# A planner's cost table replaced by durations read from a trace, in a one-core attention and feed-forward kernel

## The chip, the cores and the metric

The kernel runs on one core of a Trainium2 chip. The metric is the device time of one execution in microseconds (us). Three runs of the kernel before gave 1211.63, 1219.78 and 1224.26 us; their median, 1219.78 us, is the time before.

## What is computed

Four batches of 448 tokens, 12 heads of 64, in float32: an attention with a sigmoid in place of the softmax, and behind it two feed-forward parts on all 1792 tokens.

```python
# attention, for each batch and head
scores = q @ k.T / sqrt(64) - log(448)
x = sigmoid(scores) @ v                         # heads side by side: [1792, 768]
# first part
xn = x / sqrt(mean(x * x) + 1e-6) * rms_g
g, val = xn @ w_gate, xn @ w_val                # [768, 1536] each
x = (g * sigmoid(g) * val) @ w_out              # [1536, 768]
# second part
h = x @ w_in                                    # [768, 2048]
out = (h - tanh(h)) @ w_out2                    # [2048, 768]
```

All weights arrive as float64 words and are turned into float32 on the chip.

## The kernel before

**Products.** Tokens stand on the free axis: a matrix product takes a 128x128 block of weights and the 448 tokens of one batch. An operand is held as two float32r parts, a high one and a low one (the rest), and a product is three matmuls: high with high, high with low, low with high (L706 to L711). Nearly all matmuls of the kernel, 4896 of about 5600, stand on line L708.

**Jobs.** The feed-forward work is a list of 142 jobs, each with a piece of six weight blocks. A job of two batches is 36 matmuls. The phases are Ag and Av (gate and value), B (`w_out`), C (`w_in`) and D (`w_out2`); first the jobs of batches 0 and 1, then those of batches 2 and 3. B and D work on groups of four hidden chunks, so that four blocks make one run into a PSUM bank; a run of Ag, Av and C has six blocks.

**Conversion of a piece** (`conv`, L339 to L403): a DMA brings 768 KB (tile `raw`, two buffers); ACT makes the lowest mantissa bits (L374); DVE makes the sign (L377); DVE or ACT drops the sign (L381 or L380); DVE rebiases the exponent (L383); DVE joins the words (L387, tile `cv`, two buffers); DVE or ACT casts to the high part (L283, tile `whl`, four buffers); DVE or GpSimd (POOL) subtracts for the low part (L400).

**Epilogues** (L649 to L678): when a run of blocks is done, ACT takes a sigmoid (L654) or a tanh (L662) of the PSUM bank, DVE multiplies, subtracts or adds (L655, L658, L663, L672), and `parts` splits the result for the next phase: a cast on ACT or DVE (L283, `unit<-unit`), a subtraction on POOL or DVE (L645).

**Attention.** Batches 0 and 1 come first, two heads at a time (scores L468 and L469, values L500 and L508). The heads of batches 2 and 3 are spread over the jobs of batches 0 and 1: scores, sigmoid in place (L475), cast (L283), low part (L540), values (L552 to L555), then the squares and their sum (L576, L583). When a batch's heads are done, `norm` (L589) forms 1/rms: PE sums (L598), DVE (L612), POOL's power (L614), DVE (L603), PE (L608), ACT (L618). `x_chunk` (L627) then scales the rows (L630 on POOL or DVE, L633 on ACT, L634 on DVE).

**What sets the order.** Nothing above is issued at once. Each piece of work is given to a `Plan` (L62) with its engines and, for each, a duration in ns and whether it holds the port that DVE and POOL share. `Plan.issue` walks the work with a clock for each engine: of the pieces whose start lies within `SOON` (300 ns) of the soonest, it takes the one named first, on the engine that can start it first (L174 to L178), and advances that engine's clock by the duration. The pieces are then issued in the order of their planned starts (L204). So the durations decide two things: on which engine a piece runs where there is a choice, and where it stands in each engine's queue. On the chip each engine runs its queue in that fixed order and waits where a result isn't there yet; the plan's times themselves are not used.

The durations come from three functions and from numbers written at the call: `act(n)` (L273), `dve(n)` (L276) and `pool(n)` (L279) for n elements per partition, and `MM` (L39) for a matmul of 448 columns.

## Time and profile before

| | |
|---|---|
| median of three runs | 1219.78 us |
| lowest and highest run | 1211.63 and 1224.26 us |
| span of the profiled execution, first to last instruction | 1208.7 us |
| matmuls (PE) busy | 1177.1 us |
| DVE busy | 1049.3 us, 1444 instructions |
| ACT busy | 567.9 us, 852 instructions |
| GpSimd (POOL) busy | 253.1 us, 162 instructions |
| granted TensorE clock, mean | 0.992 of full speed (2.4 GHz) |

The whole time of the profiled execution isn't listed, only its span; the lowest run lies 2.9 us above that span, the median 11.1 us. PE is the engine of the matmuls, and their ends are modelled, so that its busy share alone doesn't tell how well it runs: how many matmuls start in a stretch tells that. A row of the timeline says when an instruction, or a merged group of them, started and how long it took; in square brackets stands for how long the engine was idle before it and who ended that.

### The profile page before, as it was taken

The numbers are of one execution on the slowest core, as the hardware profiler recorded it, in microseconds if no ns is written. First come the engines' busy times: TensorE is split into PE (matmuls) and PEld (weight loads), VectorE is DVE, ScalarE is ACT, GpSimd is POOL, SyncE is SP. The second block draws the span as 40 slices with busy tenths as digits, with TensorE's granted clock in tenths as the row PEclk, the third lists the DMA queues.
The fourth block names the chain that finished last, engine by engine and source line by source line (L and its number), as shares of the span: only waits on it lengthen the run. The fifth ranks groups of instructions, "written<-read, shape, count | busy, mean of one in ns | idle before, by whom it ended". The sixth has DMA issues, their size and how long they took to land.

```text
span 1208.7 us, 15035 instructions
## 1 busy us (share of the span) xinstructions
PE 1177.1 (97%) x5694; PEld 1042.7 (86%) x5694; DVE 1049.3 (87%) x1444; ACT 567.9 (47%) x852; POOL 253.1 (21%) x162
## 2 busy tenths in 40 slices
PE   8999999999997999999999899999999999999998
PEld 4566799989896998898899899999999999999997
DVE  4898899899999898999997999888878899888872
ACT  6876535554642566556554433243343344433330
POOL 0102312023223231222122402202212111111120
PEclk9999999999998999999999999999999999999999
DMA  7655233433333233433354243333333234332312
GB/s 253 221 190 173 69 125 137 140 115 115 126 133 111 69 111 116 137 118 106 105 171 145 84 165 105 131 106 130 105 107 107 74 105 135 127 105 105 109 49 91
DMA packets 39223, 148.86 MB, mean 123 GB/s; under 512 B 4592, under 2 KB 14064, under 8 KB 39152
## 3 DMA queue, kind: packets, MB, share of 16 engines
q1 hardware_dynamic: 39152, 147.92, 35.6%
q8 instruction: 44, 0.72, 0.2%
q14 instruction: 27, 0.22, 0.1%
HBM read 139.64 MB, written 8.26 MB: 122 GB/s over the span
## 4 chain that ended last, share of the span: by engine, by line
PE 59%; DVE 27%; ACT 6%; issue 5%; DMA 2%; POOL 1%; SPq 0%; DVEq 0%; POOLq 0%; ACTq 0%
PE ps L708 53%; DVE raw L383 4%; DVE raw L381 3%; DVE cv L387 3%; DVE unit L540 3%; DVE cv L377 2%; ACT raw L380 2%; DVE unit L645 2%; DVE unit L283 2%; PE ps L500 2%; PE ps L468 1%; PE ps L469 1%; DMA qkr<-in_qkt 1%; ACT cv L374 1%; ACT unit L283 1%
## 5 line engine op out<-in xcount | busy, mean ns | idle before, releaser
L708 PE MATMUL ps<-unit,whl 128*128 128x448 f32 x4680 | 971.7, 366 | 8.9 <-ACT unit L283 3.0
L708 PEld LDWEIGHTS ps<-unit,whl 128*128 128x128 f32 x4680 | 880.3, 188 | 83.2 <-DVE unit L540 5.0
L400 POOL TENSOR_TENSOR whl<-cv,whl 128x768 fp32r<-128x768 f32 x79 | 152.5, 1930 | 643.6 <-DVE whl L283 338.8
L374 ACT ACTIVATE cv<-raw 128x768 uint16<-128x768 uint16 x136 | 148.8, 1096 | 209.0 <-DVE whl L400 81.0
L383 DVE TENSOR_SCALAR raw<-raw 128x768 uint16<-128x768 uint16 x136 | 149.2, 1097 | 31.4 <-ACT raw L380 28.2
L387 DVE SCALAR_TENSOR_TENSOR cv<-raw,cv 128x768 uint32<-128x768 uint32 x136 | 143.4, 1054 | 7.9
L283 ACT CAST unit<-unit 128x448 fp32r<-128x448 f32 x99 | 55.0, 568 | 141.6 <-DVE unit L658 79.9
L381 DVE TENSOR_SCALAR raw<-raw 128x768 uint16<-128x768 uint16 x106 | 115.8, 1093 | 3.4
L645 DVE TENSOR_TENSOR unit<-unit 128x448 fp32r<-128x448 f32 x130 | 102.2, 803 | 16.2 <-ACT unit L283 12.5
L377 DVE TENSOR_SCALAR cv<-raw 128x768 uint16<-128x768 uint16 x136 | 92.3, 679 | 20.9 <-POOL whl L400 20.2
L672 DVE TENSOR_TENSOR unit<-ps,unit 128x448 f32<-128x448 f32 x120 | 70.1, 620 | 22.4 <-PE ps L708 22.1
L283 ACT CAST whl<-cv 128x768 fp32r<-128x768 f32 x65 | 54.4, 838 | 73.9 <-PE ps L708 51.6
L468 PE MATMUL ps<-qk 128*128 128x448 f32 x192 | 77.4, 403 | 2.6 <-DVE qk L451 1.4
L469 PE MATMUL ps<-unit,qk 128*128 128x448 f32 x192 | 71.0, 370 | 1.1 <-DVE unit L438 1.0
L475 ACT ACTIVATE ps<-ps 128x448 f32<-128x448 f32 x96 | 52.6, 549 | 27.1 <-PE ps L469 26.9
L540 DVE TENSOR_TENSOR unit<-ps,unit 128x448 fp32r<-128x448 f32 x96 | 59.7, 622 | 6.3 <-ACT unit L283 5.2
L380 ACT ACTIVATE raw<-raw 128x768 bf16<-128x768 bf16 x30 | 58.0, 1943 | 14.9 <-DVE cv L377 14.9
L468 PEld LDWEIGHTS ps<-qk 128*128 128x128 f32 x192 | 35.0, 182 | 27.0 <-issue 15.1
L662 ACT ACTIVATE unit<-ps 128x448 f32<-128x448 f32 x64 | 31.4, 543 | 55.9 <-PE ps L708 55.8
L708 PE MATMUL ps<-unit 128*128 128x448 f32 x216 | 51.1, 383 | 2.8 <-DVE unit L634 2.4
L475 ACT ACTIVATE unit<-ps 128x448 f32<-128x448 f32 x84 | 43.4, 547 | 19.2 <-PE ps L469 18.5
L708 PEld LDWEIGHTS ps<-unit 128*128 128x128 f32 x216 | 40.8, 193 | 12.8 <-issue 4.3
(65 smaller groups left out, 842.1 us busy)
## 6 DMA issues: line engine op xcount, KB each, us to landing
raw<-in_w_out SPq DMA_DIRECT2D x56, 768.0 KB, 4.3
raw<-in_w_in SPq DMA_DIRECT2D x32, 768.0 KB, 4.3
qkr<-in_qkt SPq DMA_DIRECT2D x46, 480.0 KB, 3.5
raw<-in_w_gate SPq DMA_DIRECT2D x24, 768.0 KB, 4.3
raw<-in_w_val SPq DMA_DIRECT2D x24, 768.0 KB, 4.3
out<-unit SPq DMA_DIRECT2D x24, 224.0 KB, 2.0
vs<-in_vp SPq DMA_DIRECT2D x12, 256.0 KB, 3.5
v<-in_vt SPq DMA_DIRECT2D x24, 128.0 KB, 2.1
```

The source lines that it names most:

```text
L283: add(engines, lambda e: (nc.scalar.copy if e == "ACT" else nc.vector.tensor_copy)(to(), of()), reads, writes)
L374: add(act(NW), lambda e: nc.scalar.activation(c16(0), low(), AF.Copy, scale=2.0 ** -13, bias=-0.49995), [r["l"]], [c["l"]])
L377: add(dve(NW, fast=True), lambda e: nc.vector.tensor_scalar(out=c16(1), in0=top(), scalar1=0x8000, scalar2=None, op0=ALU.bitwise_and), [r[ ...
L381: top(BF16), top(BF16), AF.Abs) if e == "ACT" else nc.vector.tensor_scalar(
L383: add(dve(NW, fast=True), lambda e: nc.vector.tensor_scalar(out=top(), in0=top(), scalar1=0x47EF, scalar2=0x3800, op0=ALU.min, op1=ALU.sub ...
L387: add(dve(NW, psum=False), lambda e: nc.vector.scalar_tensor_tensor(out=c.tile, in0=r.tile[:, :, 1], scalar=3, in1=c.tile, op0=ALU.logical ...
L400: add({**dve(wide, psum=False), **pool(wide)}, lambda e, q=q: ENG[e].tensor_sub(ap(q, "l"), f32(q), ap(q, "h").bitcast(F32)), [c["l"], c[" ...
L468: nc.tensor.matmul(ps.tile[:n, :S], lhsT=k, rhs=qk.tile[:, :S], start=(i == 0), stop=False)
L475: add(act(S, psum=True), lambda e: nc.scalar.activation(to.tile[:n, :S], ps.tile[:n, :S], AF.Sigmoid, bias=-math.log(S), scale=1.0 / math. ...
L540: add(dve(S), lambda e: nc.vector.tensor_sub(lo(), sv(), hi().bitcast(F32)), [ps["t"], kh], [kl])
L645: add({**pool(S), **dve(S, psum=False)}, lambda e: ENG[e].tensor_sub(c["l"].tile, t.tile, c["h"].tile.bitcast(F32)), [t["t"], kh], [kl])
L708: nc.tensor.matmul(ps.tile[:, :S], lhsT=wt, rhs=a[p].tile, start=first and i == 0, stop=last and i == 2,)
```

## The change

All durations that the plan goes by are set anew; the comments are taken out as well, without moving a line. The work that is given to the plan, its order of priority and the planning itself stay as they were.

```diff
-MM = 190          # ns of a matrix product of 448 columns
+MM = 203
     def act(n, psum=False, ptr=False):
-        return {"ACT": ((51 if psum else 93) + n / 1.2 + 93 * ptr, False)}
+        return {"ACT": ((165 if psum else 195) + n / 1.2 + 93 * ptr, False)}
     def dve(n, two=True, psum=True, fast=False):
-        return {"DVE": (66 + n / 0.96 / (2 if fast else 1), fast or (two and not psum))}
+        return {"DVE": (155 + n / 0.96 / (2 if fast else 1), fast or (two and not psum))}
     def pool(n):
-        return {"POOL": (110 + n * 2.16, True)}
+        return {"POOL": (570 + n * 1.77, True)}
...
-            add(act(NW), lambda e: nc.scalar.activation(c16(0), low(), AF.Copy, scale=2.0 ** -13, bias=-0.49995),
+            add({"ACT": (1100, False)}, lambda e: nc.scalar.activation(c16(0), low(), AF.Copy, scale=2.0 ** -13, bias=-0.49995),
-            add(dve(NW, fast=True), lambda e: nc.vector.tensor_scalar(
+            add({"DVE": (680, True)}, lambda e: nc.vector.tensor_scalar(
-            add({**dve(NW, fast=True), **act(NW)}, lambda e: nc.scalar.activation(
+            add({"DVE": (1095, True), "ACT": (1940, False)}, lambda e: nc.scalar.activation(
-            add(dve(NW, fast=True), lambda e: nc.vector.tensor_scalar(
+            add({"DVE": (1095, True)}, lambda e: nc.vector.tensor_scalar(
-            add(dve(NW, psum=False), lambda e: nc.vector.scalar_tensor_tensor(
+            add({"DVE": (1055, True)}, lambda e: nc.vector.scalar_tensor_tensor(
...
-            cost = 4 * MM + 60
+            cost = 1000
-            cost = 4 * MM
+            cost = 750
...
-        add({"PE": (1500, False)}, sums, [sq["t"]], [ps["t"]], stream="norm")
+        add({"PE": (950, False)}, sums, [sq["t"]], [ps["t"]], stream="norm")
-        add({"POOL": (950, True)}, lambda e: nc.gpsimd.tensor_tensor(out=rc.tile, in0=ms.tile, in1=expo, op=ALU.pow),
+        add({"POOL": (1200, True)}, lambda e: nc.gpsimd.tensor_tensor(out=rc.tile, in0=ms.tile, in1=expo, op=ALU.pow),
-        add({"DVE": (760, True)}, spread, [rc["t"]], [dg["t"]])
-        add({"PE": (1500, False)}, rows, [dg["t"]], [ps2["t"]], stream="norm")
+        add({"DVE": (1100, True)}, spread, [rc["t"]], [dg["t"]])
+        add({"PE": (900, False)}, rows, [dg["t"]], [ps2["t"]], stream="norm")
...
-        add({"DVE": (596, True)}, lambda e: nc.vector.scalar_tensor_tensor(
+        add({"DVE": (680, True)}, lambda e: nc.vector.scalar_tensor_tensor(
```

With NW = 768 the plan's charge to DVE for the four steps L377, L381, L383 and L387 of a piece goes from 3 x 466 + 866 = 2264 ns to 680 + 1095 + 1095 + 1055 = 3925 ns. A cast of 768 elements goes from 466 to 555 ns on DVE and from 733 to 835 on ACT; a low part of 768 from 866 to 955 ns on DVE and from 1769 to 1929 on POOL.

All engines keep their work but for what has a choice. Over the whole program these go from one engine to another:

| work | engine: before, now |
|---|---|
| low part of a piece, L400 (768) | POOL 79, 35; DVE 51, 95 |
| high part of a piece, L283 (768) | ACT 65, 30; DVE 65, 100 |
| high part of a result, L283 (unit<-unit) | ACT 99, 62; DVE 37, 74 |
| sign dropped, L380 or L381 | ACT 30, 41; DVE 106, 95 |
| copies from PSUM, L283 | ACT 48, 72; DVE 36, 12 |
| low part of a result, L645 | POOL 6, 14; DVE 130, 122 |

DVE has 58 instructions more, POOL 38 fewer, ACT 20 fewer. They aren't spread evenly: between the norms of batches 1 and 2 DVE has 322 instructions where it had 345, between those of batches 2 and 3 it has 344 as before, and behind the norm of batch 3, in the last 550 us, 693 where it had 612. There the low parts of pieces go from 47 on POOL and 24 on DVE to 12 and 61, the casts of pieces from 33 on ACT and 38 on DVE to 7 and 66, the casts of results on DVE from 21 to 51, L381 from 56 to 47, the copies from PSUM on DVE from 10 to none, L645 on DVE from 73 to 69; L377, L383 and L387 stand there 73 times each where they stood 70 times, since three pieces more are converted behind that norm than ahead of it.

Three places show how the queues change. The first is PE's queue at the norm of batch 2 (L552 is the last product with values of that batch, L598 the sum of its squares, L608 the spread of 1/rms). Before:

```order
L708 MATMUL ps<-unit,whl 128x448 x18
L552 MATMUL ps<-unit,vs 128x448
L708 MATMUL ps<-unit,whl 128x448 x24
L598 MATMUL ps<-ones,unit 112x1 x4
L708 MATMUL ps<-unit,whl 128x448 x12
L608 MATMUL ps<-dg,ones 128x112 x4
L468 MATMUL ps<-qk 128x448
L469 MATMUL ps<-unit,qk 128x448
```

and now:

```order
L708 MATMUL ps<-unit,whl 128x448 x18
L552 MATMUL ps<-unit,vs 128x448
L708 MATMUL ps<-unit,whl 128x448 x36
L598 MATMUL ps<-ones,unit 112x1 x4
L468 MATMUL ps<-qk 128x448
L469 MATMUL ps<-unit,qk 128x448
L708 MATMUL ps<-unit,whl 128x448 x18
L468 MATMUL ps<-qk 128x448
L469 MATMUL ps<-unit,qk 128x448
L708 MATMUL ps<-unit,whl 128x448 x6
L608 MATMUL ps<-dg,ones 128x112 x4
```

The sum stands 36 matmuls behind the last values, where it stood 24, and the spread 28 behind the sum, where it stood 12. The sum's last addition (L583) has gone from POOL to DVE.

The second is DVE's queue where batches 0 and 1 go from their last C chunk to their last D group. L663 forms the chunk's result for the two batches, L645 its low part; PE has 18 matmuls of D to do before it wants them. L634 belongs to the rows of batches 2 and 3. Before:

```order
L377 TENSOR_SCALAR cv<-raw 128x768
L381 TENSOR_SCALAR raw<-raw 128x768
L383 TENSOR_SCALAR raw<-raw 128x768
L387 SCALAR_TENSOR_TENSOR cv<-raw,cv 128x768
L283 CAST whl<-cv 128x768
L663 TENSOR_TENSOR unit<-ps,unit 128x448 x2
L645 TENSOR_TENSOR unit<-unit 128x448 x2
L634 SCALAR_TENSOR_TENSOR unit<-unit,g_sb 128x448 x2
```

and now (of the first two L663 the first is of the chunk ahead, the second and the last one are of the last chunk):

```order
L663 TENSOR_TENSOR unit<-ps,unit 128x448 x2
L383 TENSOR_SCALAR raw<-raw 128x768
L645 TENSOR_TENSOR unit<-unit 128x448
L387 SCALAR_TENSOR_TENSOR cv<-raw,cv 128x768
L283 CAST whl<-cv 128x768
L400 TENSOR_TENSOR whl<-cv,whl 128x768
L645 TENSOR_TENSOR unit<-unit 128x448
L663 TENSOR_TENSOR unit<-ps,unit 128x448
L645 TENSOR_TENSOR unit<-unit 128x448
L634 SCALAR_TENSOR_TENSOR unit<-unit,g_sb 128x448
```

The last chunk's results of the two batches stood side by side, behind a whole conversion; now the rest of a conversion and its low part stand between them.

The third is the same passage of batches 2 and 3, near the end of the program, again DVE's queue. Before:

```order
L387 SCALAR_TENSOR_TENSOR cv<-raw,cv 128x768
L283 CAST whl<-cv 128x768
L663 TENSOR_TENSOR unit<-ps,unit 128x448 x2
L645 TENSOR_TENSOR unit<-unit 128x448 x2
L283 CAST whl<-cv 128x768
L663 TENSOR_TENSOR unit<-ps,unit 128x448 x2
L645 TENSOR_TENSOR unit<-unit 128x448 x2
L672 TENSOR_TENSOR unit<-ps,unit 128x448 x12
```

and now:

```order
L283 CAST unit<-unit 128x448
L663 TENSOR_TENSOR unit<-ps,unit 128x448 x3
L377 TENSOR_SCALAR cv<-raw 128x768
L381 TENSOR_SCALAR raw<-raw 128x768
L383 TENSOR_SCALAR raw<-raw 128x768
L387 SCALAR_TENSOR_TENSOR cv<-raw,cv 128x768
L283 CAST whl<-cv 128x768
L400 TENSOR_TENSOR whl<-cv,whl 128x768
L645 TENSOR_TENSOR unit<-unit 128x448 x2
```

All conversions were done when the last chunk came; now a whole conversion with its low part stands between the last chunk's results (the last two of the three L663) and their low parts (L645), and more conversions follow.

## Rows read from the trace of the kernel before

**Rows 1.** The page: its first line, and the busy time, the share of the span and the number of instructions of three engines.

```profile
span 1208.7 us, 15035 instructions
...
PE 1177.1 (97%) x5694; PEld 1042.7 (86%) x5694; DVE 1049.3 (87%) x1444; ACT 567.9 (47%) x852; POOL 253.1 (21%) x162
```

**Rows 2.** The windows view, four stretches from the norm of batch 1 on: the stretch and its length, busy us and number of instructions of PE, PEld, DVE, ACT and POOL, the granted clock, the DMA share and GB/s.

```profile
116.00:388.00 272.00, 258.14 (x1256) 234.01 (x1255) 254.89 (x346) 136.09 (x212) 71.98 (x46) 0.98 0.35 122
388.00:652.00 264.00, 258.11 (x1265) 235.34 (x1265) 242.91 (x344) 149.66 (x231) 60.75 (x42) 0.99 0.34 118
652.00:700.00 48.00, 44.89 (x217) 40.78 (x216) 41.83 (x58) 20.47 (x30) 17.58 (x11) 0.96 0.27 95
700.00:1200.00 500.00, 500.00 (x2469) 463.32 (x2468) 417.98 (x554) 178.03 (x229) 88.23 (x46) 1.00 0.32 109
```

**Rows 3.** The waits view of PE, its longest: who waited for whom, us in total, how often, the longest.

```profile
PE ps L598 <- POOL unit L583: 8.0, 1, 8.0
PE ps L708 <- ACT unit L283: 3.0, 1, 3.0
PE ps L708 <- DVE unit L540: 2.9, 5, 1.0
PE ps L708 <- DVE unit L663: 2.9, 2, 1.5
PE ps L708 <- DVE unit L634: 2.4, 1, 2.4
```

**Rows 4.** The timeline at the norm of batch 2: start us, us, engine, line, operation, tiles, count, and the idle time before it.

```profile
372.44 2.42 DVE L383 TENSOR_SCALAR raw<-raw 128x768 uint16<-128x768 uint16 x1
...
373.60 0.19 PEld L552 LDWEIGHTS ps<-unit,vs 128*128 128x128 f32 x1
...
383.26 0.62 DVE L569 TENSOR_TENSOR unit<-ps,unit 64x448 f32<-64x448 f32 x1
...
385.01 1.93 POOL L583 TENSOR_TENSOR unit<-unit 128x448 f32<-128x448 f32 x1
...
386.99 1.65 PE L598 MATMUL ps<-ones,unit 128*112 128x1 f32 x8 [7.96 <-POOL unit L583]
```

**Rows 5.** The groups by line over the whole span: line, engine, operation, tiles, form, count, then busy us and mean ns of one, then the idle time before them.

```profile
L400 POOL TENSOR_TENSOR whl<-cv,whl 128x768 fp32r<-128x768 f32 x79 | 152.5, 1930 | 643.6 <-DVE whl L283 338.8 <-ACT whl L283 221.6 <-DVE unit L672 64.1
L645 DVE TENSOR_TENSOR unit<-unit 128x448 fp32r<-128x448 f32 x130 | 102.2, 803 | 16.2 <-ACT unit L283 12.5
L400 DVE TENSOR_TENSOR whl<-cv,whl 128x768 fp32r<-128x768 f32 x51 | 50.1, 983 | 1.4 <-ACT whl L283 0.4
L283 DVE CAST whl<-cv 128x768 fp32r<-128x768 f32 x65 | 37.4, 575 | 8.5 <-PE ps L708 7.2
L283 DVE CAST unit<-unit 128x448 fp32r<-128x448 f32 x37 | 21.0, 568 | 1.3
```

**Rows 6.** The timeline of DVE where POOL is idle, 700 to 716 us: a row of two L672, an L634 and an L630 with what follows each, and a whole conversion on DVE alone.

```profile
700.24 1.15 DVE L672 TENSOR_TENSOR unit<-ps,unit 128x448 f32<-128x448 f32 x2
...
702.76 0.68 DVE L634 SCALAR_TENSOR_TENSOR unit<-unit,g_sb 128x448 fp32r<-128x448 f32 x1
703.36 0.62 DVE L630 TENSOR_TENSOR unit<-unit 128x448 f32<-128x448 f32 x1
703.90 0.62 DVE L377 TENSOR_SCALAR cv<-raw 128x768 uint16<-128x768 uint16 x1
...
711.20 0.60 DVE L377 TENSOR_SCALAR cv<-raw 128x768 uint16<-128x768 uint16 x1
711.84 1.04 DVE L381 TENSOR_SCALAR raw<-raw 128x768 uint16<-128x768 uint16 x1
712.92 1.04 DVE L383 TENSOR_SCALAR raw<-raw 128x768 uint16<-128x768 uint16 x1
714.07 0.96 DVE L387 SCALAR_TENSOR_TENSOR cv<-raw,cv 128x768 uint32<-128x768 uint32 x1
...
715.06 0.56 DVE L283 CAST whl<-cv 128x768 fp32r<-128x768 f32 x1
715.65 0.96 DVE L400 TENSOR_TENSOR whl<-cv,whl 128x768 fp32r<-128x768 f32 x1
```

**Rows 7.** The timeline at the passage from the last C chunk of batches 0 and 1 to D.

```profile
669.67 11.26 POOL L630 TENSOR_TENSOR unit<-unit 128x448 f32<-128x448 f32 x7
...
671.63 1.56 DVE L377 TENSOR_SCALAR cv<-raw 128x768 uint16<-128x768 uint16 x1
...
678.46 1.48 DVE L283 CAST whl<-cv 128x768 fp32r<-128x768 f32 x1
...
679.86 1.14 DVE L663 TENSOR_TENSOR unit<-ps,unit 128x448 f32<-128x448 f32 x2
...
681.12 3.14 PE L708 MATMUL ps<-unit,whl 128*128 128x448 f32 x7 [3.05 <-ACT unit L283]
```

**Rows 8.** The timeline at the same passage of batches 2 and 3, where PE doesn't wait.

```profile
1175.53 0.98 ACT L662 ACTIVATE unit<-ps 128x448 f32<-128x448 f32 x2 [4.87 <-PE ps L708]
...
1176.21 1.15 DVE L663 TENSOR_TENSOR unit<-ps,unit 128x448 f32<-128x448 f32 x2
...
1176.86 1.10 ACT L283 CAST unit<-unit 128x448 fp32r<-128x448 f32 x2 [0.35 <-DVE unit L663]
1177.47 1.84 DVE L645 TENSOR_TENSOR unit<-unit 128x448 fp32r<-128x448 f32 x2
```

## The prediction

> **What bounds the kernel now.** I read the page first: PE is busy for 97% of the span, DVE for 87% [rows 1]. So the question is where PE, the engine of the matmuls, starts fewer of them than it can. The windows view tells that. From 700 to 1200 us it starts 2469 matmuls in 500 us, one each 0.2025 us, at full granted clock [rows 2]; that is the pace to hold the other stretches against. From 116 to 388 us 1256 matmuls would take 254.3 of 272 us: 17.7 us lost. From 388 to 652 us 1265 would take 256.2 of 264: 7.8 lost. From 652 to 700 us 217 would take 43.9 of 48: 4.1 lost. Together 29.6 us, all while the heads of batches 2 and 3 run beside the jobs or their rows are made. In the last 500 us nothing is lost. That is the most that a better order can win behind 116 us; ahead of it short matmuls and the start's loads don't let the same sum be made.
>
> Who is waited for: the waits view of PE names POOL and DVE, and ACT behind DVE, never a transfer [rows 3]. The largest wait, 8.0 us, is at the norm of batch 2. Its timeline shows why [rows 4]: the last values' product starts at about 373.8 us, DVE adds them up only at 383.26, POOL ends the sum of squares at 386.94, PE goes on at 386.99. DVE was some nine microseconds behind its queue, while PE stood at an instruction put in its queue too early. A plan that charges 2264 ns for four steps that in fact take 0.64 + 1.08 + 1.15 + 0.99 = 3.86 us from start to start [rows 6] must think DVE idle where it is late. So the change strikes at the cause of these waits.
>
> **The change part by part.** Nothing is computed less. What moves is who does it, and when.
>
> *The norm of batch 2, and the heads' low parts (116 to 388 us).* The sum now stands 36 matmuls behind the last values, 7.3 us, where it stood 24, 4.9 us. DVE has 23 instructions fewer in this stage, L583 no longer waits for POOL. I take 7 of the 8 us as gone (bounds 0 and 8.0). Of the other 9.7 us, 2.4 are at L634 [rows 3], where the queues stand nearly as before; of the remaining 7.3 I take half. Gain 10.5 us, bounds 0 and 17.7.
>
> *388 to 652 us.* DVE keeps 344 instructions. It was busy for 242.9 of 264 us, 92%; if PE lost nothing here, the same work would fill 95% of 256 us [rows 2]. So the gain can only come from the order. I take half: 4 us, bounds 0 and 7.8.
>
> *The first passage from C to D.* Before, DVE's conversion ahead of the last chunk ran while POOL did seven L630: from the start of L377 to that of L663 it took 679.86 - 671.63 = 8.23 us [rows 7], where the same five steps take 715.65 - 711.20 = 4.45 us with POOL idle [rows 6]. PE waited for 3.05 us. Now the conversion's end stands between the two results of the last chunk: L383 1.15, L645 twice 0.58 (as half of two L672), L387 0.99, cast 0.59, L400 0.96, together 4.85 us [rows 6]. Undisturbed, the way from the tanh to the second cast takes 1175.53 to 1177.96, 2.43 us [rows 8]; with 4.85 us more it is 7.3, and PE covers 18 matmuls, 3.65 us. Wait: 3.6 us. So this one isn't won, it only changes its cause.
>
> Behind it comes a new one. From PE's end of the fourth D run to the last operand of Ag for batches 2 and 3 DVE's queue now holds 29 instructions: six L672 at 0.58, seven L634 at 0.60, four L630 at 0.54, three L377 at 0.64, three L381 at 1.08, two L383 at 1.15, two L387 at 0.99, two L400 at 0.96 [rows 6], in sum 21.2 us; PE has 83 matmuls in the same piece of its queue, 16.8 us. That is 4.4 us late. Together 8.0 where 4.1 were lost: 3.9 us worse. Bounds: 4.1 us better if DVE catches up, 10 worse if POOL's five L630 stretch these steps as they did before (3.8 us in 4.45).
>
> *The last passage from C to D.* A whole conversion, 0.64 + 1.08 + 1.15 + 0.99 + 0.59 + 0.96 = 5.4 us [rows 6], now stands between the last chunk's two results and their low parts. Before, tanh to the end of the low parts took 1175.53 to 1179.31, 3.8 us, of which about 0.7 is POOL's doing (two L645 took 1.84 where two instructions of this size take 1.15) [rows 6, 8], and PE, with 20 matmuls to do, 4.05 us, didn't wait. Now 3.1 + 5.4 = 8.5 us stand against 4.3: 4.1 us lost. Bounds 0 and 6.
>
> *The rest of the last 550 us.* This is where the added work goes: 28 casts of pieces at 0.575, 37 low parts at 0.983, 30 casts of results at 0.568 [rows 5] are 69.5 us, and three more pieces' L377, L383, L387 at 2.78 us [rows 6] are 8.3; taken away are nine L381 at 1.08, ten copies at 0.58 and four L645 at 0.803, 18.7 us. DVE was busy there for 41.8 + 418.0, about 460 us of 548 [rows 2]: it comes to 519, 95%, hidden behind PE as long as it is spread evenly. POOL's help falls by 35 low parts of 1.93 us [rows 5], and with it the time for which POOL holds DVE up, so 519 is rather too much. I take 1 us lost, bounds 0 and 20.
>
> Here the Trainium skill speaks against the new numbers. Its page "Perfetto Trace Analysis", section "Optimizing Scalar/DVE Operations", says that a profiled duration is about twice an instruction's fixed cost, because the second half overlaps with the next one; by its 60 ns the old table was right and the new one makes DVE look fuller than it is. The trace agrees in part: two L672 take 1.15 us, not 1.23 [rows 6]. For a piece it doesn't: its four steps start 3.86 us apart in sum, near the new 3.93 and far from the old 2.26. By the rule, 95 ns off each of the 41 instructions at the three late places are 3.9 us, and the sum would be -9.4 us.
>
> *The first 116 us* keep their order but for a few swaps; 0, bounds -2 and 2.
>
> Sum: -10.5 - 4 + 3.9 + 4.1 + 1 = -5.5 us. The span goes from 1208.7 to about 1203. The execution's whole time isn't known, and the three runs lie 2.9 to 15.6 us above that span; I take the sum off their median: 1219.8 - 5.5 = 1214.3 us, -0.5%. With runs 1% apart, about 1% is what a measurement can tell here from no change.
>
> **The rivals.**
>
> *DVE isn't late at the three places, and the heads' waits go as well.* Then 17.7, 7.8 and 4.1 us shrink to some 5 in all: 25 us off, 1195 us. For it: DVE idled on PE and ACT ahead of these places before, and two-source instructions start sooner one after the other than the table says. Against it: an engine runs its queue in order, and the three sums take the shortest steps that the trace shows.
>
> *DVE becomes the bound behind the norm of batch 3.* Its place are the 16 C jobs there: a conversion of 5.4 us, two L663 and two low parts at 0.58, two casts at 0.57 make 8.9 us on DVE [rows 5, 6] against 36 matmuls, 7.3 us. If only the signs that ACT takes (26 of 73, 0.4 us a job) are off DVE, each job is 1.2 us late, 19 us in all; with 3.9 and 4.1, and 10 us won instead of 14.5, that is 17 us more: 1237 us. It decides from the point where less than 1.6 us a job is done elsewhere. Against it: 12 of 73 low parts stay on POOL there and 23 of 74 casts of results on ACT, 0.16 and 0.3 us a job more, and the B and D jobs, with three L672 and a conversion at 7.1 us, let DVE catch up.
>
> *The heads' waits are POOL's doing and stay.* Where POOL works, DVE's SBUF instructions last longer (L377 1.56 us for 0.60) [rows 6, 7]; POOL has 86 instructions in these two stages where it had 88. Then only the norm is won, 7 us, against 9 lost: 1222 us, no change.
>
> **How the numbers follow.** Forecast 0.46, the first rival 0.26, the second 0.18, the third 0.10. Faster by over 1% means below 1207.6: nearly all of the first rival and a little of the forecast, 0.29. Slower by over 1% means above 1232: most of the second rival, 0.15. The rest, 0.56, is within 1%. The forecast's own range is 1206 to 1224; to hold 8 in 10 it has to reach to the first rival and most of the way to the second: 1195 to 1232 us.
>
> **What would show it.** Right: PE's wait at L598 of batch 2 below 2 us; from 116 to 652 us fewer than 12 us lost at 0.2025 us a matmul; a wait of PE of 3 to 5 us for L663's cast at the first passage from C to D, one at L634 some 80 matmuls later, and one at L645 near the end; DVE's busy share behind the norm of batch 3 near 93%. Wrong: no wait of PE in the last 500 us, which is the first rival, or a pace there below one matmul each 0.2025 us spread over the C jobs, which is the second.

## The result and the profile after

The changed kernel takes 1227.54 us (median of 16 runs, 1223.26 to 1234.63); the kernel before takes 1219.26 us in runs beside it (16 runs, 1210.09 to 1224.26). The ratio on record is 1.0103, 95% interval 1.0077 to 1.0128: 1% slower, where 0.5% faster was forecast. The two medians alone are 0.7% apart, since before's runs fall into two groups some 10 us apart, which the part on the pace of the matmuls takes up. The profiled execution has a span of 1227.2 us, 18.5 more than before's [rows 1]. The page of after, first line and busy times:

```profile
span 1227.2 us, 14916 instructions
...
PE 1190.1 (97%) x5694; PEld 1044.8 (85%) x5694; DVE 1049.8 (86%) x1502; ACT 561.3 (46%) x832; POOL 171.7 (14%) x124
```

DVE has 58 instructions more and is busy as long as before; POOL works 81 us less. That alone tells nothing of the end. The windows view of after, same stretches and columns as [rows 2]:

```profile
116.00:388.00 272.00, 265.82 (x1294) 241.36 (x1293) 238.44 (x332) 142.03 (x227) 65.47 (x45) 0.99 0.34 117
388.00:652.00 264.00, 253.17 (x1224) 228.00 (x1223) 235.01 (x332) 141.47 (x226) 58.20 (x40) 0.99 0.34 115
652.00:700.00 48.00, 44.90 (x218) 40.89 (x217) 43.08 (x64) 17.14 (x24) 11.97 (x9) 0.96 0.37 124
700.00:1200.00 500.00, 491.47 (x2377) 448.08 (x2376) 435.26 (x615) 173.57 (x203) 22.59 (x15) 0.99 0.31 108
```

At the prediction's 0.2025 us a matmul: 1294 take 262.0 us, 10.0 lost (before 17.7); 1224 take 247.9, 16.1 lost (before 7.8); 218 take 44.1, 3.9 lost (4.1); 2377 take 481.3, 18.7 lost (0). In sum 19.1 us worse, near the 18.5 by which the spans differ. So a gain of 7.7 us came ahead of 388 us, and behind it 26.8 us were lost anew.

The waits view of PE, after, against [rows 3] (who waited for whom, us, times, longest):

```profile
PE ps L468 <- DVE unit L540: 6.0, 4, 2.0
PE ps L708 <- DVE unit L672: 5.2, 4, 2.4
PE ps L708 <- DVE unit L645: 4.6, 2, 4.3
PE ps L708 <- DVE unit L634: 3.3, 2, 2.6
PE ps L708 <- ACT unit L283: 3.1, 1, 3.1
PE ps L468 <- DVE unit L672: 3.0, 2, 2.2
```

The wait at L598 is gone. In its place attention's scores (L468) wait for DVE for up to 2.2 us, where before no such wait was longer than 1.1. The timeline of after shows how, PE and DVE at 457 to 464 us (columns as in [rows 4]):

```profile
457.14 0.36 PE L468 MATMUL ps<-qk 128*128 128x448 f32 x1
...
457.75 0.37 PE L555 MATMUL ps<-unit,vs 128*128 128x448 f32 x1
457.95 0.36 PE L468 MATMUL ps<-qk 128*128 128x448 f32 x1
...
459.35 0.65 DVE L540 TENSOR_TENSOR unit<-ps,unit 128x448 fp32r<-128x448 f32 x1
459.93 0.93 DVE L387 SCALAR_TENSOR_TENSOR cv<-raw,cv 128x768 uint32<-128x768 uint32 x1
460.05 0.47 PE L468 MATMUL ps<-qk 128*128 128x448 f32 x1 [1.13 <-DVE unit L540]
...
460.89 0.56 DVE L283 CAST whl<-cv 128x768 fp32r<-128x768 f32 x1
461.49 0.96 DVE L400 TENSOR_TENSOR whl<-cv,whl 128x768 fp32r<-128x768 f32 x1
462.48 0.62 DVE L540 TENSOR_TENSOR unit<-ps,unit 64x448 fp32r<-64x448 f32 x1
463.15 0.63 PE L468 MATMUL ps<-qk 128*64 128x448 f32 x1 [2.02 <-DVE unit L540]
```

Scores and values of one key chunk after another stand in PE's queue with no job's matmuls between them. Each L468 needs a PSUM bank that L540 empties, and L540 stands in DVE's queue behind a piece's conversion (L387, cast, L400: 2.5 us). In the queue of after there are three runs of 17 attention matmuls behind the norm of batch 1; before there is one of six, at 132 us, and else none of more than four.

### The profile page after: what moved, and what is told of

Same layout as the page of the kernel before. It is cut to its first block, busy times and chain, and to the rows that moved or that the text cites. A ratio compares the mean times of both kernels' runs of the same rounds, so it can differ in the third digit from the quotient of the medians.

```text
span 1227.2 us, 14916 instructions
## 1 busy us (share of the span) xinstructions
PE 1190.1 (97%) x5694; PEld 1044.8 (85%) x5694; DVE 1049.8 (86%) x1502; ACT 561.3 (46%) x832; POOL 171.7 (14%) x124
## 4 chain that ended last, share of the span: by engine, by line
PE 78%; DVE 15%; DMA 3%; ACT 2%; issue 1%; POOL 0%; DVEq 0%; POOLq 0%; ACTq 0%; SPq 0%
PE ps L708 71%; DMA qkr<-in_qkt 3%; PE ps L468 2%; PE ps L469 2%; DVE raw L383 2%; DVE cv L387 1%; DVE unit L645 1%; DVE raw L381 1%; DVE whl L400 1%; PE ps L500 1%; DVE unit L672 1%; DVE cv L377 1%; PE ps L555 1%; PE ps L554 1%; DMA raw<-in_w_in 1%
## 5 line engine op out<-in xcount | busy, mean ns | idle before, releaser
L383 DVE TENSOR_SCALAR raw<-raw 128x768 uint16<-128x768 uint16 x136 | 144.3, 1061 | 13.1 <-ACT raw L380 10.7
L400 POOL TENSOR_TENSOR whl<-cv,whl 128x768 fp32r<-128x768 f32 x35 | 65.3, 1866 | 576.1 <-DVE whl L283 458.0
L387 DVE SCALAR_TENSOR_TENSOR cv<-raw,cv 128x768 uint32<-128x768 uint32 x136 | 132.6, 975 | 4.5
L381 DVE TENSOR_SCALAR raw<-raw 128x768 uint16<-128x768 uint16 x95 | 104.2, 1097 | 3.0
L400 DVE TENSOR_TENSOR whl<-cv,whl 128x768 fp32r<-128x768 f32 x95 | 95.2, 1002 | 5.6 <-ACT whl L283 3.1
L377 DVE TENSOR_SCALAR cv<-raw 128x768 uint16<-128x768 uint16 x136 | 93.8, 690 | 2.2 <-DMA raw<-in_w_gate 2.1
L672 DVE TENSOR_TENSOR unit<-ps,unit 128x448 f32<-128x448 f32 x120 | 70.3, 622 | 29.2 <-PE ps L708 29.0
L380 ACT ACTIVATE raw<-raw 128x768 bf16<-128x768 bf16 x41 | 80.2, 1957 | 23.1 <-DVE cv L377 23.0
L468 PE MATMUL ps<-qk 128*128 128x448 f32 x192 | 79.0, 412 | 11.5 <-DVE unit L540 6.0
L645 DVE TENSOR_TENSOR unit<-unit 128x448 fp32r<-128x448 f32 x122 | 80.8, 669 | 6.3 <-ACT unit L283 3.9
L662 ACT ACTIVATE unit<-ps 128x448 f32<-128x448 f32 x64 | 32.2, 549 | 81.9 <-PE ps L708 81.8
L468 PEld LDWEIGHTS ps<-qk 128*128 128x128 f32 x192 | 35.2, 183 | 37.7 <-issue 15.6
L540 DVE TENSOR_TENSOR unit<-ps,unit 128x448 fp32r<-128x448 f32 x96 | 59.5, 623 | 8.3 <-ACT unit L283 7.3
L283 DVE CAST whl<-cv 128x768 fp32r<-128x768 f32 x100 | 60.2, 602 | 5.0
L283 ACT COPY unit<-ps 128x448 f32<-128x448 f32 (+1 forms) x72 | 36.6, 536 | 54.1 <-PE ps L708 48.8
L283 ACT CAST unit<-unit 128x448 fp32r<-128x448 f32 x62 | 34.6, 567 | 47.2 <-DVE unit L658 17.1
L451 POOL TENSOR_TENSOR qk<-qkr,qk 64x448 fp32r<-64x448 f32 (+1 forms) x23 | 30.3, 1318 | 150.7 <-ACT qk L283 106.4
```

Source lines behind the costliest of these rows:

```text
L283: add(engines, lambda e: (nc.scalar.copy if e == "ACT" else nc.vector.tensor_copy)(to(), of()), reads, writes)
L377: add({"DVE": (680, True)}, lambda e: nc.vector.tensor_scalar(out=c16(1), in0=top(), scalar1=0x8000, scalar2=None, op0=ALU.bitwise_and), [ ...
L381: top(BF16), top(BF16), AF.Abs) if e == "ACT" else nc.vector.tensor_scalar(
L383: add({"DVE": (1095, True)}, lambda e: nc.vector.tensor_scalar(out=top(), in0=top(), scalar1=0x47EF, scalar2=0x3800, op0=ALU.min, op1=ALU. ...
L387: add({"DVE": (1055, True)}, lambda e: nc.vector.scalar_tensor_tensor(out=c.tile, in0=r.tile[:, :, 1], scalar=3, in1=c.tile, op0=ALU.logic ...
L400: add({**dve(wide, psum=False), **pool(wide)}, lambda e, q=q: ENG[e].tensor_sub(ap(q, "l"), f32(q), ap(q, "h").bitcast(F32)), [c["l"], c[" ...
```

## The experiments

The 15 runs below are told by what they part. "PE lost" is, from the norm of batch 1 on, the sum over all steps from one matmul to the next of more than 0.26 us, each less 0.203 us, from the run's trace. "Share" and "idle" are no measurement: they are read off the plan that the program makes, from the norm of batch 1 to the last matmul: DVE's charged time as a share, and the time for which the plan itself leaves PE without work. The diffs are given in short.

**Which numbers do it?** The conversion's five alone, then all the others alone.

```diff
 # conv_only: before, with
+L374 1100, L377 680, L381 1095 or L380 1940, L383 1095, L387 1055
 # rest_only: the changed kernel, without these
```

> The kernel before with the new numbers of the five conversion steps alone (L374, L377, L380 and L381, L383, L387). Theory 1: these numbers make the loss, since they make DVE look full in the plan between 116 and 652 us, so that the attention's work falls behind there and its matmuls are put into PE's queue in bursts, behind which PE waits for a PSUM bank that DVE is to free (L468 or L708 behind L540 or L672). The queue that they give on PE has runs of up to 17 attention matmuls, as the changed kernel's has (before: never over 4). Then the ratio to before is 1.005 to 1.014, PE's waits in the 264 us between the norms of batches 2 and 3 are 14 us or more (before 9.0, changed 17.7). Rival, theory 2: the new charges for the other work (act, dve, pool, MM) make it; then the ratio is 0.997 to 1.003.

> The changed kernel with the five conversion steps charged as before; all other new numbers stay. Theory 1 (the conversion's numbers make the loss): the queue on PE has no run of over 4 attention matmuls, PE's waits between the norms of batches 2 and 3 stay at 7 to 11 us and the ratio to before is 0.996 to 1.003. Theory 2 (the other charges make it): ratio 1.005 to 1.014 and 14 us of waits or more there.

Measured: 1222.56 us, ratio 1.0068 (1.0040 to 1.0096), and 1206.23 us, 0.9954 (0.9920 to 0.9988). The conversion's numbers make the loss; the others make a small gain, just beyond theory 1's range (rest_only lost 3.7 us between the norms of batches 2 and 3, where theory 1 had 7 to 11). But of conv_only's 46.8 us lost only 12.7 lie between the norms of batches 2 and 3, less than theory 1 wanted; 18.8 lie behind 850 us, where DVE's casts come late, as PE's waits from 700 us on show:

```profile
PE ps L708 <- DVE unit L283: 7.1, 4, 3.7
```

**Are durations the fault, or larger numbers as such?** A DVE instruction ends in the trace after the next has begun: an L540 of after that starts at 449.46 us lasts 0.62 us, and the next instruction starts at 450.00, 0.54 later. all_ss charges such steps from start to start everywhere; conv_ss does so for the conversion alone.

```diff
 # all_ss: before, with MM 203 and
+L374 960, L377 640, L381 1080 or L380 1690, L383 1080, L387 880
+dve: (195 if fast else 70) + ...      pool: 570 + 1.77 n
+norm and values on PE 950, 900, 1000, 750; power 1200
 # conv_ss: before, with the first of these lines alone
```

> All charges as the trace shows the step from one instruction's start to the next on a full queue, in place of the durations: conversion 960, 640, 1080 or 1690, 1080 and 880; DVE 70 ns beside its elements, 195 for the fast form; POOL 570 ns and 1.77 ns an element; MM 203; ACT as before. Theory A: the loss comes from charging durations, which overlap from one instruction to the next by 80 to 250 ns, so that DVE looks fuller than it is; then there are hardly any bursts (the longest run of attention matmuls is 6), one of the late places behind 652 us stays, the wait at the norm of batch 2 (8.0 us) is gone, and the ratio to before is 0.985 to 0.998. Rival B: any larger number for the conversion makes bursts and late conversions; the ratio is then 1.003 to 1.012.

> The kernel before with the five conversion steps alone charged as the step from start to start (960, 640, 1080 or 1690, 1080, 880), and MM still at 190. It parts the two readings of the run in which all charges were steps from start to start: theory F (a full DVE in the plan; here 0.85 to 0.91 behind the norm of batch 1, with PE idle for 39 us in the plan, two runs of 17 attention matmuls and two late places, 2.9 and 2.8 us) gives 0.999 to 1.006 and waits of 8 us or more between the norms of batches 2 and 3; theory A (durations are wrong, steps from start to start are right for the conversion) gives 0.985 to 0.995.

Measured: all_ss 1194.73 us, 0.9843 (0.9800 to 0.9886), just below theory A's range. conv_ss 1211.13 us, 0.9976 (0.9943 to 1.0008), between the two theories, with 10.9 us lost between the norms of batches 2 and 3 as F had it. So the truer number for the conversion isn't enough by itself. all_ss differs from the changed kernel in ACT's charges too, which it leaves as before. No run parts the two, but the plans do: the changed kernel with ACT's old charges still has PE idle for 84 us in the plan (85 with the new), and all_ss with ACT's new ones for 26 (20 without). So it is DVE's charges that fill the plan.

**Is it the full DVE of the plan?** Only PE's charge is changed, to more than the trace shows.

```diff
 # after_mm240 / after_mm225: the changed kernel, with
-MM = 203
+MM = 240      # and 225
 # ss_mm215: all_ss, with
-MM = 203
+MM = 215
```

> The changed kernel with one number more changed: a matmul is charged 240 ns (MM) in place of 203, which the trace shows to be too much (202.7 or 206.7). Theory F: what costs is that the plan holds DVE, with the port it shares with POOL, for its fullest engine (in the changed kernel's plan DVE is charged 0.87 to 0.90 of every stretch behind the norm of batch 1, and the plan itself leaves PE idle for 87 us behind there; before 0.62 to 0.77 and 5 us). DVE's steps then stand no further ahead of PE than they must, and PE's attention matmuls come in bursts. With 240 ns the plan's DVE is at 0.71 to 0.83, its PE idle for 4 us, the queue has no run of over 4 attention matmuls and no late conversion. Then PE waits for under 8 us behind the norm of batch 1 (changed kernel 46 us, before 32) and the ratio to before is 0.975 to 0.992. Rival G: the new charges themselves do the harm (DVE's share against ACT and POOL, the sharing out of the steps), and a wrong PE charge can't mend it: ratio 1.000 to 1.012.

> The changed kernel with a matmul charged at 225 ns, between its own 203 (ratio 1.0103) and 240 (0.9894). Theory F: the plan's own PE idle behind the norm of batch 1 is 13 us (87 with 203, 4 with 240), with one run of 17 attention matmuls and two late places of 2.0 and 0.6 us; the time lies between, near the lower one: ratio 0.988 to 0.997. Rival G (the charges do the harm, and 240 ns only happened to fit): no order in the three values, 0.998 to 1.012.

> All charges as steps from start to start, but a matmul at 215 ns in place of 203: by order alone no late conversion is left and no run of over 4 attention matmuls, and the plan leaves PE idle for 4.6 us behind the norm of batch 1 (22 with 203). Theory F: PE's waits behind the norm of batch 1 fall from about 11 to under 5 us, the ratio is 0.972 to 0.985, at or below the 0.984 with 203. Rival G (a truer PE charge is better): ratio 0.985 to 0.995. Since a stretch without waits keeps its pace of 202.67 or 206.66 ns, single runs should lie in two groups some 10 us apart, as before's do.

Measured: after_mm240 1198.36 us, 0.9894 (0.9846 to 0.9942); after_mm225 1188.04 us, 0.9794 (0.9750 to 0.9837); ss_mm215 1189.61 us, 0.9819 (0.9769 to 0.9869). One number turns the 1% loss into a gain of 1 to 2%, so rival G falls for the changed kernel. ss_mm215 has F's ratio, but it lost 11.5 us, hardly less than all_ss (12.4), where F had under 5; the intervals of the two ratios overlap, so F and G aren't told apart there. But 225 is better than 240, not between 203 and 240 as F said, and after_mm240 loses 16.6 us where F had under 8. Its two largest waits of PE behind the norm of batch 1 are of the kind that before had:

```profile
PE ps L598 <- DVE unit L583: 5.0, 2, 4.6
PE ps L708 <- ACT unit L283: 3.0, 1, 3.0
```

A plan that has too much time for DVE (share 0.78) puts PE's instructions in too early, as before did (0.71). So the loss has two sides. What after_mm225 makes of the first two stretches of [rows 2], the windows view:

```profile
116.00:388.00 272.00, 270.69 (x1345) 248.61 (x1344) 252.64 (x353) 146.45 (x220) 83.53 (x58) 1.00 0.36 121
388.00:652.00 264.00, 262.81 (x1294) 239.65 (x1293) 248.79 (x354) 145.56 (x229) 59.40 (x42) 1.00 0.35 121
```

1345 matmuls stand where before had 1256 and after 1294, and 1294 where they had 1265 and 1224. DVE is busy for 94% in the second of them, and hardly holds PE up. This kernel has one run of 17 attention matmuls as well, from 541 us on; by the measure of "PE lost" it costs 2.0 us, where the three runs of the changed kernel with the waits right behind them cost 19.1. So a long run isn't a loss of that size by itself. What else DVE's queue holds between the run's own steps seems to decide, which no run shows apart: a piece's L387, cast and L400 at 460 us above, an L387 alone here.

**The sharing out, or the order?** The engine of each step with a choice is fixed to that of the other kernel (WHO, a list read off its plan).

```diff
 # after_eng: the changed kernel, engines of before; before_eng: the reverse
-for e, (ns, uses_port) in engines.items():
+for e, (ns, uses_port) in [x for x in engines.items() if len(engines) == 1 or x[0][0] == WHO[n]]:
```

> The changed kernel's charges and so its order, but every step that has a choice stays on the engine that it has in the kernel before (POOL 79 low parts of pieces, DVE 58 instructions fewer than changed). Theory F (the order that a full DVE gives): the plan still holds DVE at 0.81 to 0.90 and leaves PE idle for 81 us behind the norm of batch 1, the queue has three runs of 17 attention matmuls and five late places; ratio to before 1.004 to 1.014. Rival H (DVE's 58 instructions more, the sharing out, do the harm): ratio 0.994 to 1.003.

> The reverse: the charges of the kernel before, with every step that has a choice on the engine that the changed kernel puts it on (DVE 58 instructions more, POOL 38 fewer). The plan leaves PE idle for 4 us behind the norm of batch 1, no run of over 4 attention matmuls, no late place. Theory F: ratio to before 0.994 to 1.003. Rival H: 1.004 to 1.014.

Measured: after_eng 1231.50 us, 1.0149 (1.0097 to 1.0200), just above F's range; before_eng 1220.79 us, 1.0054 (1.0024 to 1.0084). Giving DVE's added work back doesn't mend the order that the new charges make: the sharing out isn't needed for the loss. (The plan is made anew with the engines fixed, so after_eng has an order of the same kind and not the very same.) But the new sharing out under the old charges lands in H's range and not in F's, so it has a price of its own: one wait of 8.8 us from 938 us on, in a row of gate and value jobs, against 7.6 us lost between the norms of batches 1 and 2 where before lost 17.9. PE's waits in before_eng from 700 us on:

```profile
PE ps L708 <- DVE unit L283: 9.7, 2, 8.8
```

**Is it the share alone, with charges that get less true?** This was open: in the runs so far the fuller plans were also the truer ones. The old charges are kept and a matmul is charged less.

```diff
 # before_mm165 / before_mm150: before, with
-MM = 190
+MM = 165      # and 150
```

> The old charges, all of them, with one number changed: a matmul at 165 ns in place of 190 (the trace shows 203). Over the runs so far the time that PE loses behind the norm of batch 1 goes with the share of the plan's time that DVE is charged there: 32 to 36 us lost at 0.71 to 0.74, 17 to 25 at 0.77, 11 to 12 at 0.83 to 0.86, 33 to 47 at 0.87 and above. Theory F2: what counts is this share alone, whether the charges are true or not; with 165 ns it is 0.84 (the plan's own PE idle 19 us), so PE loses 10 to 18 us and the ratio to before is 0.978 to 0.990. Rival T (truth): the old table is wrong among DVE, ACT and POOL, and a matmul charged still further from the truth makes it worse: 1.000 to 1.012.

> The old charges with a matmul at 150 ns: DVE's share of the plan is 0.87, its own PE idle 61 us, the queue has runs of up to 17 attention matmuls and four late places of 1.9 to 6.4 us, as with the changed charges. Theory F2: the far side of the same curve, PE loses 30 to 48 us, ratio 0.998 to 1.012; it is then the full DVE that makes the bursts and late places, with old charges as with new ones. Rival T: worse than 165 ns as well, but without the turn between them, 1.005 to 1.02 and above 165 by little.

Measured: before_mm165 1203.44 us, 0.9879 (0.9835 to 0.9922), 19.9 us lost (two more than expected); before_mm150 1232.93 us, 1.0115 (1.0069 to 1.0161), 52.0 us lost (four more). Both sides of the turn come out with the old table, which charges an L381 466 ns where the trace steps on after 1080, and rival T falls. Whether the truth of the charges counts for something beside is not shown: before_mm165 and all_ss have the same share and idle time and lost 19.9 and 12.4 us, but the intervals of their ratios overlap. At 150 ns PE's longest waits are those of the changed kernel:

```profile
PE ps L708 <- DVE unit L283: 7.6, 2, 4.1
PE ps L708 <- DVE unit L672: 6.8, 1, 6.8
PE ps L708 <- DVE unit L634: 4.0, 4, 2.0
PE ps L708 <- DVE unit L540: 4.0, 4, 2.6
```

All orders side by side:

| kernel | share | idle, us | PE lost, us | ratio to before |
|---|---|---|---|---|
| before | 0.71 | 3 | 32.2 | 1 |
| before_eng | 0.74 | 2 | 35.8 | 1.0054 |
| rest_only | 0.77 | 5 | 24.9 | 0.9954 |
| after_mm240 | 0.78 | 2 | 16.6 | 0.9894 |
| ss_mm215 | 0.83 | 3 | 11.5 | 0.9819 |
| before_mm165 | 0.84 | 19 | 19.9 | 0.9879 |
| all_ss | 0.85 | 20 | 12.4 | 0.9843 |
| after_mm225 | 0.86 | 11 | 10.6 | 0.9794 |
| after_eng | 0.86 | 79 | 52.1 | 1.0149 |
| conv_ss | 0.87 | 37 | 33.0 | 0.9976 |
| before_mm150 | 0.87 | 61 | 52.0 | 1.0115 |
| conv_only | 0.88 | 77 | 46.8 | 1.0068 |
| the change | 0.88 | 85 | 46.8 | 1.0103 |

The time goes with the time that PE loses. That is large where the plan thinks DVE has a quarter of its time free, and again where the plan itself leaves PE idle for more than some 35 us. after_eng shows that the idle time tells the far side better than the share. On the near side neither number tells all: rest_only and after_mm240 are alike in both and lost 24.9 and 16.6.

**The pace of the matmuls.** In after's profile 1283 matmuls from 722 to 987 us start 206.66 ns apart, all others of the last 500 us, waits and what follows them aside, 202.67; in before's all 2563 from 685 us on start 202.67 apart. The place at which it changes back, 987.6 us, is a step of 0.71 us, a short wait. To see what a matmul of another size does, nine matmuls of the second half were written as two.

```diff
 # split8: before; after_split: the changed kernel; ss215_split, mm225_split: the orders above
+cut = [0, 224, 448] in every 8th job of batches 2 and 3, second block, else [0, 448]
+for lo, hi in zip(cut, cut[1:]): matmul of columns lo to hi
```

> The kernel before with one matmul in every eighth job of the second half (jobs of batches 2 and 3, 9 places) written as two of 224 columns each; nothing else moves. It asks what sets the two paces of a 448-column matmul at the full granted clock (202.67 and 206.66 ns), of which a run of some 2560 matmuls without a wait seems to keep one or the other to its end, 10 us apart. Theory P: the pace can change at any matmul of another size; then the last 500 us show both paces, the runs lie between the two groups of before's runs (1210 to 1213 and 1219 to 1224 us) and their spread is smaller. Rival Q: it changes at a wait of PE alone; then the runs fall into the same two groups, 1 to 2 us higher, and one execution has one pace from 690 us to the end. If there are no two paces but only some other disturbance, the profile shows intervals that change with no place.

> The changed kernel with one matmul in every eighth job of the second half written as two of 224 columns, which held the pace at 202.67 ns in both kernels that had it. It takes the pace out of the loss: what is left above before with the same places (1211.5 us, 0.997 of before) is that of waits alone. If some 1300 of the changed kernel's matmuls behind 720 us ran at 206.66 ns in most of its runs, as in its profile, it gains 3 to 7 us: 1220 to 1225 us, ratio 1.004 to 1.010, and the runs lie within 6 us of one another (changed kernel: 11). If the pace has no part in it: ratio 1.009 to 1.013.

> The same plan with 215 ns, and one matmul in every eighth job of the second half written as two of 224 columns. If a matmul of another size puts the pace back to 202.67 ns, the runs lie within 5 us of one another, as in the first run with such places, and at the fast group of the same plan without them: 1182 to 1190 us, ratio 0.970 to 0.982. If the split only draws the pace anew, the spread is 5 to 10 us about the mean of the two groups.

> The best order so far (the changed charges, a matmul at 225 ns) with the nine split matmuls. The profile of that order had 202.67 ns from 692 us to the end, so if the split only takes the slow pace out, the fastest runs stay and the spread falls below 4 us: 1185 to 1190 us, ratio 0.975 to 0.982.

Measured: split8 1209.20 to 1214.45 us in 12 runs, ratio 0.9971 (0.9943 to 0.9999), where before's 29 runs beside it fall into 1208.3 to 1215.3 and 1220.0 to 1223.2. That is neither P, with runs between the groups, nor Q, with both groups: the upper group is gone. ss215_split 1188.50 to 1190.52 us, 0.9805 (0.9762 to 0.9849), where ss_mm215's six runs are 1187.28 to 1189.73 and 1198.18 and 1198.72; the profiled one is of the upper group. Windows of ss_mm215, then of ss215_split (to compare: the count of matmuls, in brackets behind PE's busy time):

```profile
750.00:850.00 100.00, 100.00 (x486) 90.81 (x485) 91.94 (x120) 31.41 (x42) 3.69 (x2) 1.00 0.33 111
1000.00:1100.00 100.00, 100.00 (x486) 90.81 (x485) 88.85 (x124) 40.67 (x43) 5.85 (x3) 1.00 0.33 111
```

```profile
750.00:850.00 100.00, 100.00 (x497) 92.72 (x496) 93.75 (x124) 31.42 (x42) 3.70 (x2) 1.00 0.35 119
1000.00:1100.00 100.00, 100.00 (x497) 92.73 (x496) 91.87 (x129) 38.21 (x42) 5.85 (x3) 1.00 0.33 111
```

PE is busy for all of it at full granted clock (2.4 GHz) in both, and starts 486 matmuls in 100 us or 497 (one or two of them halves). In the profiles with splits, every row of 287 matmuls between two of them ran at 202.7 ns. So the splits keep the slow pace out, they don't draw it anew. In none of the four profiles does a row at 206.66 ns run into a split, so that a split turns the pace back is argued from the runs' times and not seen. after_split missed its time: 1227.07 us, 1.0111 (1.0061 to 1.0161), in the range that stood for a pace without a part in the loss, its runs within 3.8 us of one another where the changed kernel's spread over 11.4. The pace widens that spread and is not the loss: after_split lost 48.5 us where split8 lost 32.2, and these 16.3 us are nearly the 15.6 between their medians (which weren't run side by side). With the slow pace out of both kernels the change thus costs some 1.3%; the two groups of before's runs hide a part of it. mm225_split, 1188.87 us (1187.89 to 1191.06), 0.9759 (0.9720 to 0.9798), is as fast as after_mm225 without the splits, which had no run of an upper group.

## Why the prediction was wrong

Five of its six terms had the right sign (the first 116 us, for which it took 0, too: the norm of batch 1 comes at 113.8 us before and at 113.3 after). The second failed. In the profiled executions the sum missed by 24 us, from -5.5 to +18.5: by 12.3 in the second term, 2.8 in the first, and some 9 behind 652 us, which no term had.

- *116 to 388 us, -10.5.* Right in sign, 2.8 us too large: 7.7 us came. The norm's wait went whole, and most of the other waits of before with it, but the first run of 17 attention matmuls, at 302 us, costs 8.9 us up to 316. The sum's last addition (L583) ends 0.57 us before PE comes to the sum, as the timeline of after shows against [rows 4], and L598 has no wait:

```profile
374.44 0.37 PE L552 MATMUL ps<-unit,vs 128*128 128x448 f32 x1
...
375.51 0.62 DVE L569 TENSOR_TENSOR unit<-ps,unit 64x448 f32<-64x448 f32 x1
...
380.21 1.16 DVE L583 TENSOR_TENSOR unit<-unit 128x448 f32<-128x448 f32 x1
...
381.94 0.85 PE L598 MATMUL ps<-ones,unit 128*112 128x1 f32 x8
```

- *388 to 652 us, -4 with bounds 0 and -7.8.* This is the step that failed: +8.3 us. "The gain can only come from the order. I take half" took a truer table to mean a better order and gave the order no way to lose; the runs of 17 in it could be read before the run. What the runs showed in its place is in the table above: charged 0.88 of its time, with the port held besides, DVE is the plan's fullest engine, and the plan itself leaves PE idle for 85 us.

  How that makes the runs of 17 can be read off the plan. Behind each of the three, the job's next block has its weights in time, but it is planned for 190 ns (the plan's time from one engine to another) after the end of a DVE step that empties a PSUM bank (L540, L663, L672); until then attention's products, most of them named further down, are put into PE's queue ahead of their turn, with nothing between them. That DVE itself had room on the chip shows in after_mm225, where the same DVE charges lose 2.9 us between the norms of batches 2 and 3 (the changed kernel 17.7, before 9.0).

  Here the Trainium skill's page "Perfetto Trace Analysis", section "Optimizing Scalar/DVE Operations", bears on the charges: it says that about half of an instruction's fixed cost, as profiled, overlaps the next instruction. The trace agrees: of the 0.62 us of an L540 0.47 are 448 elements at the plan's 0.96 an ns, and of the other 0.15 us half is gone in the step of 0.54. The prediction's use of that rule, -9.4 us, missed by more. It asked only when DVE would be done on the chip, and took the 95 ns off steps that were read from start to start and so held the overlap already; what the durations did to the plan it left out. all_ss, charged by the steps that the trace shows, is 1.6% faster than before.

- *The first passage from C to D and the chain behind it, 3.6 and 4.4 us of waits.* Right in place and cause, mis-sized in the second: 3.1 and 2.6 us. The cast of the last L663 comes behind a conversion, as the order said; against [rows 7]:

```profile
678.98 0.96 DVE L400 TENSOR_TENSOR whl<-cv,whl 128x768 fp32r<-128x768 f32 x1
...
680.39 0.62 DVE L663 TENSOR_TENSOR unit<-ps,unit 128x448 f32<-128x448 f32 x1
681.04 0.56 ACT L283 CAST unit<-unit 128x448 fp32r<-128x448 f32 x1 [3.54 <-DVE unit L663]
...
681.66 0.74 PE L708 MATMUL ps<-unit,whl 128*128 128x448 f32 x1 [3.10 <-ACT unit L283]
```

- *The last passage, 4.1 us.* Right: 4.3 us (8.5 less the 4.05 or 4.3 of the text is 4.2 to 4.5, not 4.1), against no wait in [rows 8]:

```profile
1188.20 1.16 DVE L663 TENSOR_TENSOR unit<-ps,unit 128x448 f32<-128x448 f32 x2 [3.44 <-ACT unit L662]
...
1195.46 1.15 DVE L645 TENSOR_TENSOR unit<-unit 128x448 fp32r<-128x448 f32 x2
...
1196.13 2.40 PE L708 MATMUL ps<-unit,whl 128*128 128x448 f32 x5 [4.29 <-DVE unit L645]
```

- *What follows a wait.* No term had it beyond what before had. After PE had stood still for 4.29 us, its granted clock was at the lower of its two levels (1.2 GHz) for nearly 4 us, and steps of 0.37 us cost some 2 us more; the same stands behind the wait of 2.59 us at L634. Behind the norm of batch 3 PE lost 18.5 us where before lost 5.3: 9.1 of the 13.2 more are waits, nearly the sum's 9.0, and 4.1 are such slow steps. The windows view of after, behind these two waits and later:

```profile
718.40:722.00 3.60, 3.60 (x11) 3.19 (x12) 3.50 (x5) 1.64 (x3) 0.00 (x0) 0.55 0.22 32
1196.20:1200.00 3.80, 3.73 (x10) 3.10 (x11) 3.70 (x5) 1.09 (x1) 0.00 (x0) 0.56 0.29 123
1200.20:1204.00 3.80, 3.80 (x21) 3.52 (x20) 1.92 (x5) 0.00 (x0) 1.85 (x1) 1.00 0.33 121
```

- *The rest of the last 550 us, 1 us.* Right as to waits: PE waits there for 1.1 us at a cast and 0.3 at another L645, and DVE isn't the bound. DVE's load was sized wrong: 43.1 + 435.3 = 478 of 548 us, 87%, where 519 and 95% were forecast. With POOL busy for 34.6 us there where it had 105.8, a cast of a result on DVE took 0.40 us on average (before 0.70) and an L645 0.63 (0.80). The 5.1 us (1283 times 4.0 ns) of the slow pace were not in the sum. They look like the second rival's mark, a pace below one matmul each 0.2025 us in the C jobs, but nobody is waited for in them.

The rival on the slower side, DVE as the bound behind the norm of batch 3, had the right engine but the wrong side: DVE is the bound in the plan, not on the chip. Of the prediction's own signs the three waits and the one at L598 came as it said; two did not, DVE's share near 93% (87%) and fewer than 12 us lost from 116 to 652 us (26.1).

## What to carry to other kernels

What follows rests on this one kernel and its 15 runs. In a list scheduler the costs don't only describe the work; their ratio decides how far each engine is run ahead. Charge what an engine is held for (start to start) rather than a profiled duration, then look at what the plan itself says: if it leaves the engine that bounds the kernel idle, raise that engine's cost until it doesn't, and stop before the others look free. And read the new order where the waits are, a run of one stream's instructions on the bounding engine above all, before giving a better table the credit of a better order.

## What the runs showed of the hardware

A matmul of 448 columns at the full granted clock has two paces, 202.67 and 206.66 ns from start to start; a long row of them keeps the one it has, over 2435 matmuls in one profile (9.7 us). The pace changed only where a step differed: at waits of PE, and in two profiles (conv_only and before_mm165) at a step of 226 and 228 ns. In the four profiles with nine split matmuls every row between two splits ran at 202.7 ns. Some 2500 matmuls at the one pace instead of the other make 10 us, which fits the groups into which the runs of one kernel fall; with such groups a median of three tells little under 1%. What sets the pace is open.
